# Sums of squares of two batches moved from ScalarE to TensorE, with a new order of all steps

## The chip, the cores and the metric

The kernel runs on one core of a Trainium2 chip. The metric is the time of one execution on the device in microseconds. Its engines each work through their own list of instructions in order: PE (TensorE) with its weight loads PEld, DVE (VectorE), ACT (ScalarE), POOL (GpSimd), and SP, whose queue issues all DMAs.

## The reference, cut to what matters

```python
def _attn_ref(q, k, v, n_global, n_local):        # 4 batches, 8 heads, 768 rows, 64 columns a head
    scores = (1.0 / np.sqrt(D)) * np.matmul(q, k.transpose(0, 1, 3, 2))
    keep = is_global | is_local                   # 8 first columns, and a band of 96
    scores = np.where(keep, scores + bias, -1e9)  # bias: slope of the head times the distance
    a = np.exp(scores - max)
    return np.matmul(a / (a.sum(-1, keepdims=True) + 1e-9), v)

def _moe_ref(x, w_in, w_out):                     # x: 3072 x 512, w_in: 512 x 2048, w_out: 2048 x 512
    h = x @ w_in
    g = h * erf(softplus(h))
    return g @ w_out
```

The weights come as 8-byte floats, q, k and v as 4-byte floats.

## The kernel before, in words

The rows are worked in 24 tiles of 128 (6 for each of 4 batches). Each tile goes through scores (step S), a penalty and row minimum on DVE (E), the exponential on ACT (X), a split into two 2-byte halves (eh, el), a transpose by DMA (et), the product with v (V), the division (x) and a split and transpose of the result (xh, xl, xt). Two tiles make a unit of 256 rows. A unit runs through four groups of 512 hidden columns: n = 0 to 95 counts quarters of them in the code's terms as (n, f), and the steps of group n are the up product (h, four parts), its eviction to SBUF (H), a chain of activations on ACT (t, l, i, G), products on DVE or POOL (P, Q, c, C), the split of the result (g, j) and the down product (d, eight parts), then the eviction of the output (O) and its store (o). ACT changes its function table between the steps t, G and the steps X, l, i.

All products are made of 2-byte halves, so each operand needs a scale, a power of two. For v, k and q it comes from the sum of squares of a batch: v_load brings a piece of a batch into the tile `vm` (steps vd, kd, qd), v_square squares it and adds up along the row (vq, kq, qq), v_sums adds over the partitions by a product with ones (vm), v_scale makes the scale (vp). Batch 0 has three pieces of v of 1024 columns, in tiles of tag H; each later batch has 18 pieces of 512 columns, six of v, k and q each, in one buffer of tag `vm`. For the weights w_in and w_out the same sum is bounded by a Gram product on PE and the maximum of its rows (wi_gram, gram_max; steps Wq and Wr).

The order is written out by hand as a table of steps, ORDER. Each engine executes its own instructions in the order in which the steps stand there; the table is one list for all engines, and a step is the call of one method (run_fast maps names to methods). A letter behind a step chooses the engine: a is ACT, v is DVE, p is POOL. PSUM has two buffers of tag `h`, which the up products, the transposes on PE and (later batches) v_sums share, and two of tag `o` for the down products. The profile gives nearly all instructions line 202, the line of the recording helper `Stamped`, so they are told apart by their tiles.

Of the kernel before, what the change touches and what calls it, by code (L numbers as in the profile page):

```python
# [74 lines left out]
el0,0,1 eP1,0,1 Qc2v E1,2,1 Ra7a Rc7p E1,2,0 vd0,1,3 Wq2 vd0,0,3 vq0,1,3 vq0,2,3 Wr2v Wm2 vq0,0,3 vm0 Wd4 eP1,0,0 Wh1v
ld0,2 vp0 vh0v Wl1 vl0 S2,0 Wi4a E2,0,1 Wp2 Wa4a Wc4a V0,0 V0,2 Rd12 Rd13 Ri12a Ri13p Wb4 eh1,0,1a X2,0,1 el1,0,1
eh2,0,1v el2,0,1p Wq4 Ra12a Rd2 Ri2p eh1,0,0v el1,0,0 x0 X1,2,1 eP1,2,1 Ra13a Rc13a Rd14 Ri14a E2,0,0 Ra2v Rb13 Rc2v
Ra14a Rd4 Wr4a Ri4v X2,0,0 eh2,0,0v Ra4a xP0 xh0a Rd5 va1 el2,0,0p Rc12v Wm4 eh1,2,1a S2,2 el1,2,1 E2,2,0 E2,2,1 Wh2p
xl0p ld1,2 vh1p Wd3 vl1 Wi3a Wa3a Wc3v X1,2,0 Rb12 ld3,1 TQ3 Rc14v Qc3a eP1,2,0 Wb3 Rb7 vd1,0,6 vq1,0,6 Wl2 eh1,2,0a
Rd3 ld3,0 TK3 Rc4a Rb4 Ri3a K3a V1,0 Wq3 Wr3v X2,2,0 eh2,2,0a el2,2,0v Wd5 Ra3a Rc3v Wm3 Wp3 Wh3p Wp4 ld2,2 vh2a kd1,0  # L80
Ri5a kq1,0 ld4,0 et2,0,1 S3,0 TK4 Rd15 E3,0,1 el1,2,0 qd1,0 Rb14 Wl3 Wi5a Wa5a Wc5a E3,0,0 X3,0,0 V1,2 x1 Wb5 Wq5
qq1,0 Ra5a Rc5v Rb5 Wr5v Wm5 K4a Rd0 Ri0a Ra0a Ri15p Ra15a xP1 Rb2 Wd6 Wi6a Wa6a vd1,1,6 Wh4p Rb6 Rq1 eh3,0,0a
el3,0,0p Wl4 Wd7 vq1,1,6 Rc15v ld5,0 Rb15 S3,2 Wi7p TK5 xh1v Wp5 xl1p h0,0 Rr1v Wz0 Wc6a Wb6 et2,2,0 Wh5v Wl5 X3,0,1
kd1,1 et2,0,0 X2,2,1 kq1,1 K5a Wa7a Wc7v Wq6 Wr6a eh3,0,1a Rm1 Rd1 Ra1v Ri1p qd1,1 Wm6 h0,2 Rc0a Rd8 el3,0,1v Wp6
H0,0a Rd9 Wb7 vl2 qq1,1 Rc1a eh2,2,1v el2,2,1p Ri8a Ra8a E3,2,0 X3,2,0 Rd10 Wq7 Ri10a vd1,2,6 vq1,2,6 Rp1 Ra10a ld4,1
Wr7v E3,2,1 Wm7 Wp7 Rb1 H0,2a Wh6p va2 Wl6 Ri9a Rc10v Ra9a TQ4 Rb10 Qc4a Rd11 V2,0 S4,0 Ri11v Ra11v Wz1 Rc11v Rb11
X3,2,1 kd1,2 kq1,2 et2,2,1 Rc8a Rb8 eh3,2,0a el3,2,0v Rc9a et3,0,0 qd1,2 Rb9 qq1,2 V2,2 eh3,2,1a el3,2,1p ld3,2 vh3a
et3,0,1 Rb3 Rb0 Rq3 Rr3a x2 xh2v xl2p vl3 Rq2 Rr2a Rm2 Rp2 Rh11p Rh9p vd1,3,6 E4,0,1 vq1,3,6 E4,0,0 va3 Wh7a Rq0 Rr0v
Rh8a X4,0,0 ld5,1 Rh10v Rl11 X4,0,1 kd1,3 kq1,3 et3,2,0 Rl10 Rh4a eh4,0,0a el4,0,0p ld4,2 Rl8 Rh6a Wl7 TQ5 Rm0 Rp0
vh4p Rh0p Rh7a S4,2 Qc5v E4,2,1 Rm3 Rp3 Rh5a qd1,3 qq1,3 et3,2,1 Rl9 h0,1 va4 H0,1a t0,0 Rl6 V3,0 V3,2 x3 Rh1a E4,2,0  # L90
Rl4 Rh15p vd1,4,6 vq1,4,6 vl4 Rl15 xt2 eh4,0,1a X4,2,1 el4,0,1v Rh3p et4,0,0 eh4,2,1a el4,2,1p kd1,4 kq1,4 Rh2v Rl5
ld5,2 h1,1 Rl0 et4,0,1 S5,0 E5,0,1 Rh12a h1,0 H1,0v E5,0,0 xh3v Rl1 X4,2,0 eh4,2,0v qd1,4 X5,0,0 Rl12 el4,2,0v et4,2,1
Rh13v X5,0,1 eh5,0,1v qq1,4 S5,2 va5 Rh14p Rl14 h0,3 l0,0 i0,0 E5,2,1 vd1,5,6 vq1,5,6 xl3v vh5v V4,0 H1,1a Rl7 G0,0
h1,2 et4,2,0 H0,3a kd1,5 kq1,5 Rl2 eh5,0,0v ld6,1 vl5 Rl3 t1,0 P0,0v Q0,0v el5,0,1p et5,0,1 H1,2a t0,1 h1,3 V4,2
# [5 lines left out]
H2,2v H2,3v X6,2,1 S7,0 j0,1 vq2,1,6 X6,2,0 eh6,2,0v h3,3 kd2,1 el6,2,0p et6,2,0 Kl8 d0,4 d0,5 d0,6 l2,0 Kt8 xh4a xl4p  # L100
h3,0 xt4 i1,1 E7,0,1 X7,0,1 C1,0 E7,0,0 x5 xh5v xl5v xt5 V6,0 kq2,1 g1,0a j1,0 t2,1 S7,2 vh7p vl7 d0,7 d1,0 d1,1 d1,2
eh7,0,1v ld9,0 eh6,2,1v el6,2,1p KF9v qd2,1 G1,1 G2,0 d1,3 H3,0v et6,2,1 V6,2 P1,1v el7,0,1v et7,0,1 Q1,1v Qh8a Ql8
c1,1 X7,0,0 eh7,0,0v el7,0,0p Qt8 qq2,1 ld9,1 l2,1 E7,2,0 X7,2,0 eh7,2,0a KC1,1p E7,2,1 X7,2,1 eh7,2,1a et7,0,0
el7,2,0p C1,1 g1,1a vd2,2,6 ld8,2 el7,2,1p et7,2,1 S8,0 E8,0,0 x6 E8,0,1 i2,0 X8,0,1 vq2,2,6 i2,1 et7,2,0 h3,1 j1,1
H3,1a V7,0 S8,2 kd2,2 Kh9p va8 Rl13 eh8,0,1a G2,1 P2,1p d1,4 Kl9 Kt9 d1,5 d1,6 P2,0v el8,0,1v Qh9v et8,0,1 Q2,0v kq2,2
qd2,2 vh8a Ql9 E8,2,0 H3,3v h4,0 E8,2,1 t3,0 t3,1 ld10,0 H4,0a X8,0,0 xh6v c2,0 xl6v Qt9 xt6 vl8 ld10,1 d1,7 O0,0a
V7,2 X8,2,0 Q2,1v eh8,0,0v h4,1 H4,1a o0,0 c2,1 X8,2,1 h4,2 eh8,2,1a el8,0,0v C2,1 et8,0,0 eh8,2,0a l3,1 el8,2,0v
et8,2,0 O0,1a ld9,2 S9,0 g2,1p E9,0,1 qq2,2 el8,2,1p et8,2,1 Qh10p E9,0,0 H4,2v h4,3 H4,3v C2,0 X9,0,0 va9 Kh10a g2,0p
Kl10 i3,1 l3,0 S9,2 E9,2,0 Kt10 x7 xh7a h5,1 Ql10 vd2,3,6 h5,0 Qt10 j2,0 i3,0 V8,0 V8,2 j2,1 ld11,1 X9,2,0 G3,0
# [1169 lines left out]
```

## Time and profile before

| | us |
|---|---|
| median of 3 runs | 679.18 (677.45 to 679.87) |
| profiled execution | 679.95 |
| its span, first to last instruction | 678.2 |
| PE, DVE, ACT, POOL busy | 628.6, 603.9, 618.8, 184.4 |
| mean granted clock of PE | 0.961 of full |

The busy time of an engine counts its instructions, with overlaps counted once. A matmul row's mean duration includes its passage through the array, so consecutive matmuls overlap: the time from one start to the next is what a matmul costs in a stream. Weight loads (PEld) run beside matmuls.

### The profile page before, as it was taken

How to read it: one execution, taken by the hardware profiler on the slowest of the kernel's cores; microseconds unless marked ns; L12 is line 12 of the kernel's file. 1: busy time of each engine (PE TensorE's matmuls, PEld its weight loads, DVE VectorE, ACT ScalarE, POOL GpSimd, SP SyncE). 2: the span in 40 equal slices, each digit the busy share in tenths (PEclk: the TensorE clock that was granted, in tenths of full speed). 3: DMA queues.
4: the chain of work that ended last, by engine and by line, in shares of the span. 5: the costliest groups of instructions: out<-in, count | busy, mean ns of one | idle time of the engine just before them, and what ended most of it. 6: DMA issues, size and time to landing. Idle time of an engine off the chain costs nothing.

```text
span 678.2 us, 13956 instructions
## 1 busy us (share of the span) xinstructions
PE 628.6 (93%) x5280; PEld 433.0 (64%) x5280; DVE 603.9 (89%) x1139; ACT 618.8 (91%) x875; POOL 184.4 (27%) x153
## 2 busy tenths in 40 slices
PE   4775789789999999999999999999999999999996
...
DVE  6999999999999999999999999889997989774863
ACT  5899998999999999999999999898998999999970
...
PEclk9856979999999999999999999999999999999999
...
GB/s 264 345 345 254 282 199 185 177 204 157 207 190 182 174 139 172 176 175 163 158 143 176 163 134 112 118 148 80 129 66 110 124 65 47 42 38 32 1 33 36
DMA packets 244668, 100.79 MB, mean 149 GB/s; under 512 B 225520, under 2 KB 225520, under 8 KB 244592
## 3 DMA queue, kind: packets, MB, share of 16 engines
...
## 4 chain that ended last, share of the span: by engine, by line
PE 60%; DVE 18%; ACT 8%; DMA 8%; issue 3%; POOL 1%; SPq 0%; DVEq 0%; ACTq 0%
PE h L202 27%; PE o L202 26%; DMA eT<-w 4%; PE po L202 3%; PE s L202 3%; DVE C L202 2%; DVE wo L202 2%; DVE e L202 2%; DVE raw_wo L202 2%; ACT B L202 2%; DVE w L202 1%; ACT A L202 1%; DVE A L202 1%; DVE B L202 1%; DMA vm<-in_q 1%
## 5 line engine op out<-in xcount | busy, mean ns | idle before, releaser
L202 PE MATMUL h<-xT,wi_hi 128*128 128x256 f16 x1536 | 257.0, 274 | 4.9 <-ACT H L202 2.5
L202 PE MATMUL o<-wo,g 128*128 128x512 f16 x1152 | 258.4, 379 | 1.8 <-ACT osb L202 1.3
L202 PE MATMUL h<-xT,wi_lo 128*128 128x256 f16 x768 | 210.1, 274 | 0.0
L202 PEld LDWEIGHTS <-g 128*128 128x128 f16 x1152 | 110.8, 98 | 128.3 <-issue 3.7
L202 PEld LDWEIGHTS <-wi_hi 128*128 128x128 f16 x1536 | 148.3, 98 | 33.7 <-issue 8.6
L202 POOL TENSOR_TENSOR w<-e,w 128x512 f16<-128x512 f32 (+1 forms) x43 | 56.9, 1326 | 177.9 <-DVE w L202 83.4
L202 ACT ACT_TABLE_LOAD x73 | 93.7, 1283 | 8.8 <-DVE wi_lo L686 7.5
L202 ACT ACTIVATE e<-e,mn 128x256 f32<-128x256 f32 (+1 forms) x192 | 81.9, 480 | 6.4 <-DVE mn L202 6.1
L202 PEld LDWEIGHTS <-wi_lo 128*128 128x128 f16 x768 | 75.4, 98 | 9.0
L202 DVE SCALAR_TENSOR_TENSOR g<-C,gs,g 128x1024 f16<-128x1024 f32 x48 | 67.0, 1399 | 6.5 <-POOL g L202 5.9
L202 DVE SCALAR_TENSOR_TENSOR C<-A,B 128x1024 f32<-128x1024 f32 x48 | 58.9, 1227 | 11.2 <-POOL B L202 10.4
L202 DVE CUSTOM_DVE_ANT_0 e<-s,pen,kqs 128x256 f32<-128x256 f32 (+1 forms) x144 | 59.3, 456 | 2.6 <-POOL w L202 2.2
L202 DVE TENSOR_TENSOR B<-C,B 128x1024 f32<-128x1024 f32 x43 | 54.7, 1272 | 7.1 <-POOL A L202 6.4
L202 DVE SCALAR_TENSOR_TENSOR C<-C,H 128x1024 f32<-128x1024 f32 x48 | 59.1, 1231 | 0.9
L202 ACT ACTIVATE A<-A,halves 128x1024 f32<-128x1024 f32 x48 | 54.7, 1141 | 0.2
L202 POOL TENSOR_SCALAR g<-C,gs 128x1024 f16<-128x1024 f32 x20 | 26.9, 1344 | 100.2 <-DVE C L202 84.2
L202 ACT ACTIVATE B<-A 128x1024 f32<-128x1024 f32 x48 | 50.8, 1057 | 2.9 <-DVE C L202 1.2
L202 ACT ACTIVATE B<-B 128x1024 f32<-128x1024 f32 x48 | 50.4, 1052 | 0.8
L202 PE MATMUL s<-kT,qT 64*128 64x256 f16 (+3 forms) x528 | 47.5, 311 | 3.7 <-ACT kT L202 1.4
L202 ACT ACTIVATE C<-A 128x1024 f32<-128x1024 f32 x48 | 49.9, 1051 | 0.3
L202 DVE TENSOR_TENSOR A<-A,B 128x1024 f32<-128x1024 f32 x38 | 46.3, 1220 | 4.1 <-ACT C L202 4.1
L202 ACT ACTIVATE A<-H 128x1024 f32<-128x1024 f32 x48 | 49.4, 1050 | 0.4
...
## 6 DMA issues: line engine op xcount, KB each, us to landing
...
```

The costliest lines, as they stand in the source:

```text
L202: i = getattr(self.engine, name)(*a, **k)
```

## The change

v_square has a second form, used for batches 0 and 1 (`SQ_ACT = 2`). It does not square on ACT; it reads the upper 2 bytes of each 4-byte float as a number of the 2-byte type bf16 (every second 2-byte word of the tile), cuts the tile into chunks of 64 columns (16 in a tile of 1024, 8 in one of 512) and multiplies each chunk by itself on PE, all into one 64 x 64 tile `gv` in a PSUM buffer of tag `h`. A new step (vr, kr, qr) takes the maximum of each of its rows on DVE. The sum over partitions then runs over 64 in place of 128. Batches 2 and 3 stay as they were. The table ORDER is written anew throughout: it has the same steps, with 21 new maxima, in other places, and many steps have another engine behind them (for example P: 38 on DVE and 10 on POOL before, 42 and 6 now; el: 45 on DVE and 43 on POOL before, 36 and 52 now; the output evictions O: 18 on ACT and 6 on DVE before, 14 and 10 now).

```diff
+SQ_ACT = 2
...
-el5,0,0v H1,3a qd1,5 qq1,5 xt3 X5,2,1 ld6,0 vm1 et5,0,0 c0,0 C0,0 g0,0a h3,2 vp1 Qh6a vd2,0,6 Kh6v Kl6 Ql6 eh5,2,1v
...
+vr0,0 ld2,0 TK2 K2v X0,2,1 vq0,2,3 Rd14 Ri14p Ra14a Wd2 Wc1p Wi2v Wa2a Wc2p eP1,0,1 eh1,0,1a Wb1 vr0,2 S1,2 E1,2,1
...
-        k = part.shape[1]
-        self.nc.tensor.matmul(ps[:, 0:k], self.ones, part, start=True, stop=True)
+        n, k = part.shape
+        self.nc.tensor.matmul(ps[:, 0:k], self.ones[0:n, :], part, start=True, stop=True)
...
     def v_square(self, b, i, k, z="v"):
+        t = self.vm.pop((b, i, z))
+        pe = self.fast and b < SQ_ACT
         if b not in self.a_v:
-            self.a_v[b] = self.small.tile([P, k if k == 3 else 3 * k], F32, tag=f"a_v{k}", bufs=3, name=f"a_v{b}")
-        t = self.vm.pop((b, i, z))
-        i += "vkq".index(z) * k
-        self.nc.scalar.activation(t, t, AF.Square, accum_out=self.a_v[b][:, i : i + 1])
+            self.a_v[b] = self.small.tile([D if pe else P, k if k == 3 else 3 * k], F32, tag=f"a_{'g' if pe else 'v'}{k}", bufs=1 if pe else 3, name=f"a_v{b}")
+        j = i + "vkq".index(z) * k
+        a = self.a_v[b][:, j : j + 1]
+        if not pe:
+            self.nc.scalar.activation(t, t, AF.Square, accum_out=a)
+            return
+        c = t.bitcast(BF16).rearrange("p (a b w) -> p a b w", b=D, w=2)[:, :, :, 1]
+        n = c.shape[1]
+        g = self.ps_h.tile([D, D], F32, tag="h", name=f"gv_{b}_{i}_{z}")
+        for m in range(n):
+            self.nc.tensor.matmul(g, c[:, m], c[:, m], start=(m == 0), stop=(m == n - 1))
+        self.gv[b, i, z] = (g, a)
+
+    def v_gram_max(self, b, i, z="v"):
+        g, a = self.gv.pop((b, i, z))
+        self.nc.vector.tensor_reduce(a, g, axis=AX.X, op=ALU.max)
```

Place 1 is PE in group 1 of the first unit, where its third up part (h_2) ends and its fourth (h_3) begins. `vm_4` is a piece of q of batch 1, `gv_4_q` its Gram tile, `xT` the input of the up product. Before:

```order
L202 LDWEIGHTS wi_lo
L202 MATMUL h_2_1519<-xT_525,wi_lo 128x256
L202 LDWEIGHTS wi_hi
L202 MATMUL h_3_1567<-xT_525,wi_hi 128x256
L202 LDWEIGHTS wi_hi
```

Now, with seven more pairs like the one shown at the dots:

```order
L204 LDWEIGHTS wi_lo
L204 MATMUL h_2_1603<-xT_596,wi_lo 128x256
L204 LDWEIGHTS vm_4_1633
L204 MATMUL gv_4_q<-vm_4_1633 64x64
...
L204 LDWEIGHTS wi_hi
L204 MATMUL h_3_1652<-xT_596,wi_hi 128x256
```

A Gram of eight pairs stands between two up parts that followed each other.

Place 2 is ACT while the last pieces of batch 1 are worked. `vm_4` and `vm_5` are pieces of batch 1, `a_v` takes their sums, A, B, C and H are tiles of the activation chain, `e` and `w` belong to the attention tile. Before:

```order
L202 ACTIVATE vm_4_1427,a_v_584<-vm_4_1427 128x512
L202 ACTIVATE A_1262<-A_1262,halves 128x1024
L202 ACTIVATE B_0_1478<-A_1262 128x1024
L202 ACTIVATE B_0_1478<-B_0_1478 128x1024
L202 ACTIVATE vm_5_1484,a_v_584<-vm_5_1484 128x512
L202 ACTIVATE H_0_1415<-h_1_1352,hs_836 128x512
L202 ACT_TABLE_LOAD
```

Now, at the same activations of the first group:

```order
L204 ACTIVATE A_1066<-A_1066,halves 128x1024
L204 ACTIVATE B_0_1587<-A_1066 128x1024
L204 ACTIVATE e_0_1_1590<-e_0_1_1590,mn_1492 128x256 x2
L204 ACTIVATE B_0_1587<-B_0_1587 128x1024
L204 ACTIVATE wo<-wo,swo 128x512
L204 ACTIVATE H_1_1628<-h_3_1652,hs_962 128x512
L204 ACT_TABLE_LOAD
```

The squares are gone from ACT's row there, and an exponential and a split of w_out stand between the same activations.

Place 3 is DVE at the same time, after the change only, where it takes the maxima of `gv_4_q` and `gv_5_v` into `a_v`. `vb`, `xw`, `w` and `wo` are splits into halves.

```order
L204 TENSOR_REDUCE a_v_576<-gv_4_q 64x1
L204 SCALAR_TENSOR_TENSOR wo<-raw_wo_738,swo,wo 128x512
L204 CAST xw_1649<-x_1567 128x512
L204 SCALAR_TENSOR_TENSOR vb_150<-vraw_5_1506,s_v_405,vb_150 128x8x64
L204 CAST w_0_1_1683<-e_0_1_1590 128x512
L204 TENSOR_TENSOR xw_1649<-x_1567,xw_1649 128x512
L204 TENSOR_TENSOR w_0_1_1683<-e_0_1_1590,w_0_1_1683 128x512
L204 SCALAR_TENSOR_TENSOR wo<-raw_wo_616,swo,wo 128x512
L204 SCALAR_TENSOR_TENSOR wo<-raw_wo_680,swo,wo 128x512
L204 TENSOR_SCALAR wo<-raw_wo_549,swo 128x512
L204 TENSOR_REDUCE a_v_576<-gv_5_v 64x1
```

The two maxima have nine other instructions between them. At the end of the program the last two output evictions, both on ACT before, stand one on ACT (o_1) and one on DVE (o_0).

## Rows read from the trace of the kernel before

**Rows 1.** Page, parts 1 and 2: busy shares, then the span in 40 slices.

```profile
PE 628.6 (93%) x5280; PEld 433.0 (64%) x5280; DVE 603.9 (89%) x1139; ACT 618.8 (91%) x875; POOL 184.4 (27%) x153
PE   4775789789999999999999999999999999999996
DVE  6999999999999999999999999889997989774863
ACT  5899998999999999999999999898998999999970
PEclk9856979999999999999999999999999999999999
```

**Rows 2.** Busy us by stretch: PE, PEld, DVE, ACT, POOL, PE clock, DMA share.

```profile
0.00:60.00 60.00, 37.87 (x244) 28.58 (x244) 51.41 (x152) 49.00 (x81) 16.76 (x25) 0.74 0.97 310
60.00:120.00 60.00, 47.97 (x422) 38.65 (x423) 57.13 (x147) 54.99 (x100) 19.09 (x17) 0.83 0.88 225
0.00:180.00 180.00, 139.71 (x1185) 105.59 (x1186) 166.90 (x427) 162.72 (x272) 52.72 (x58) 0.86 0.89 238
180.00:640.00 460.00, 458.31 (x3934) 311.61 (x3932) 416.69 (x696) 437.19 (x586) 127.18 (x93) 1.00 0.58 124
```

**Rows 3.** Chain that ended last: page part 4, then pieces (start, us, what).

```profile
PE 60%; DVE 18%; ACT 8%; DMA 8%; issue 3%; POOL 1%; SPq 0%; DVEq 0%; ACTq 0%
100.47 4.24 PE h L202 x24
104.71 1.46 PE po L202 x48
106.17 2.62 PE h L202 x24
```

**Rows 4.** Instruction groups by shape on ACT and DVE: busy us, mean ns, idle before.

```profile
L202 ACT ACTIVATE vm<-vm 128x1024 f32<-128x1024 f32 x3 | 3.1, 1065 | 0.0
L202 ACT ACTIVATE vm<-vm 128x512 f32<-128x512 f32 x54 | 33.6, 622 | 3.0 <-DMA vm<-in_q 2.1 <-DMA vm<-in_k 0.5 <-DMA vm<-in_v 0.2
L202 ACT ACTIVATION_READ_ACCUMULATOR vm<-vm 128x1 f32 x57 | 10.8, 190 | 0.0
L202 DVE TENSOR_REDUCE as_v<-pt_v 128x3 f32<-128x18 f32 x3 | 0.5, 169 | 0.0
L202 DVE TENSOR_REDUCE a_wi<-gr_wi 128x1 f32<-128x256 f32 x6 | 2.5, 417 | 0.0
L202 ACT ACT_TABLE_LOAD x73 | 93.7, 1283 | 8.8 <-DVE wi_lo L686 7.5
L202 ACT ACTIVATE H<-h,hs 128x512 f32<-128x512 f32 x62 | 41.0, 675 | 6.2 <-PE h L202 6.2
L202 DVE TENSOR_SCALAR H<-h,hs 128x512 f32<-128x512 f32 x34 | 25.0, 746 | 5.7 <-PE h L202 5.4
```

**Rows 5.** Timeline of PE at 74 us: start, us, instructions.

```profile
74.11 1.11 PE L202 MATMUL gr_wi<-wo 128*128 128x128 bf16 x8
76.03 0.38 PE L202 MATMUL h<-xT,wi_hi 128*128 128x256 f16 x2
```

**Rows 6.** Weight loads by shape: busy us, mean ns, idle before.

```profile
L202 PEld LDWEIGHTS <-wi_hi 128*128 128x128 f16 x1536 | 148.3, 98 | 33.7 <-issue 8.6 <-DMA xT<-xw 1.1 <-DVE xT L202 1.0
L202 PEld LDWEIGHTS <-wo 128*128 128x128 bf16 x80 | 8.6, 122 | 8.5 <-DVE wo L202 8.4
```

**Rows 7.** Waits (total us, times, longest), and tile vm up to 180 us.

```profile
PE h L202 <- ACT H L202: 2.5, 2, 2.3
  ACT vm L202: 2.0, 4
DMA to landing us min/median/max: 2.7/3.2/7.8
```

**Rows 8.** Timeline at the end: start, us, instructions, idle before.

```profile
667.29 4.92 PE L202 MATMUL o<-wo,g 128*128 128x512 f16 x22 [0.34 <-DVE g L202]
672.25 1.26 ACT L202 ACTIVATE osb<-o,gs 128x512 f32<-128x512 f32 x2 [12.16 <-PE o L202]
```

More of the change, by code (lines that the diff above doesn't have):

```diff
@@ L75 @@
[L75 to L94, printed above, removed]
@@ L100 @@
[L100 to L109, printed above, removed]
@@ new lines @@
+Rd15 Ri15a vd0,1,3 vq0,1,3 ld2,1 Ra15a Rc15a vr0,1 el1,0,1 ld0,2 vm0 vp0 TQ2 eP0,2,1 Qc2a E1,2,0 ld1,2 vh1v Wq1 Wr1a
+Wm1 S2,0 X1,2,0 vh0p vl0 Wb2 Wp1 Wh1p V0,0 Wq2 X1,2,1 eP1,2,1 eh1,2,1a eh0,2,1v el0,2,1 V0,2 eP1,0,0 eh1,0,0a Rd12
+Wr2v Wm2 E2,0,0 X2,0,0 E2,0,1 X2,0,1 el1,2,1 Rd4 x0 Wp2 vd1,0,6 Ri4p el1,0,0 eh2,0,1a eP1,2,0 eh1,2,0a el1,2,0 Rd0
+Ri0p Ra0a Rc0v Wl1 KF3p Ri12p Ra12a Rd6 Ri6a S2,2 Ra6v Wd3 Wi3a Wa3a Rd1 Wc3a va1 vq1,0,6 vl1 xP0 vr1,0 Rc14p Ra4a
+el2,0,1v xh0v kd1,0 Ra1a Rb14 Wd4 kq1,0 kr1,0 E2,2,1 Rd7 X2,2,1 V1,0 Wb3 E2,2,0 Rc4a X2,2,0 Rc12v Rb12 Rb0 Ri1p Rc1v
@@ new lines @@
+ld3,1 TQ3 ld2,2 Ri7a Ra7a Wq3 Wi4v Wr3a Rd5 eh2,0,0v el2,0,0p xl0v Ri5a Wm3 Wp3 Wh3v eh2,2,1a el2,2,1v Wh2v qd1,0
+qq1,0 qr1,0 Wl2 Rc7v Rb7 vh2a vl2 Wa4a Wc4a Wb4 ld3,0 Ra5a TK3 K3a Rb4 Wl3 Qc3a S3,0 Rd13 E3,0,1 Ri13a Ra13v Wd5 Wi5a
+Wa5a Wc5a vd1,1,6 vq1,1,6 vr1,1 E3,0,0 V1,2 et2,2,1 x1 Wb5 eh2,2,0a el2,2,0v S3,2 Rc13p Wd6 Rb13 Wi6a Rc5a Wa6a ld4,0
+TK4 Rc6v et2,0,0 Rb6 xP1 E3,2,0 Wq5 K4v Wq4 Wr5a Wr4a xh1a xl1p X3,2,0 Wm4 Wp4 Wm5 et2,0,1 Wp5 va2 V2,0 ld4,1 TQ4 Qc4a
+Wc6p Wb6 kd1,1 Rb15 X3,0,0 eh3,0,0a Rb1 kq1,1 kr1,1 Wh5a Wh4a h0,0 el3,0,0p eh3,2,0a el3,2,0p Wd7 Wz0 Wl5 E3,2,1 h0,2
@@ new lines @@
+H0,0a qd1,1 qq1,1 Wi7a Wa7v X3,2,1 qr1,1 Wc7v Rd2 et2,2,0 Wq6 Rd10 X3,0,1 Wr6a eh3,0,1a Ri2v vd1,2,6 Wb7 h0,1 Ri10a
+Ra10v Rb5 Wl4 H0,1a t0,0 Wm6 Rd11 Ra2a V2,2 ld3,2 vh3p Rd3 vq1,2,6 H0,2v kd1,2 S4,0 x2 E4,0,1 Wq7 Wr7a Wp6 Wm7 Wp7
+vr1,2 Rd8 Rd9 el3,0,1p Rc2a E4,0,0 X4,0,0 kq1,2 kr1,2 Ri3p Ra3a Ri8a Rc10a Rb2 Ri11a vl3 Ri9a Ra9a h1,0 Wz1 Rc3v Rb3
+qd1,2 qq1,2 qr1,2 H1,0a et3,0,0 Ra8v Rc8v Rb8 Rq3 Rr3a ld5,0 xh2a Rq1 Rr1a vd1,3,6 vq1,3,6 Wh6p TK5 et3,2,0 S4,2 Wl6
+Ra11a Wh7a vr1,3 Rb10 Rc9v Rb9 Rc11v xl2v Rb11 Wl7 eh3,2,1a el3,2,1v K5a et3,0,1 h0,3 H0,3a kd1,3 kq1,3 kr1,3 Rm1
```

199 lines of the change are left out of this document (108 added, 91 removed).

## The prediction

> **What bounds the kernel now.** I read the views from coarse to fine. The page's header and slices first [rows 1]: three engines carry almost the same load, PE 93%, ACT 91% and DVE 89% of the span, so nothing stands out by its share. The sums by stretch second [rows 2]: from 180 to 640 us PE is busy 458.3 of 460 us, at full clock. In the first 180 us it is busy 139.7, so 40.3 us of its idle time lie there, while DVE works 166.9 and ACT 162.7 of 180. So the front is bound by ACT and DVE, the middle by PE (which needs ACT and DVE close behind it, at 95% and 91%), and the end is short. The chain that ended last, third [rows 3]: 60% PE, 18% DVE, 8% ACT, 8% DMA. A microsecond taken from ACT in the front is worth something only if DVE, just as full there, gets shorter too; this is why the new layout of all parts counts as much as the new operation.
>
> **Removed.** 21 squares on ACT: 3 tiles of 1024 columns at 1.065 + 0.190 us and 18 of 512 columns at 0.622 + 0.190 us [rows 4], 3.8 + 14.6 = 18.4 us. All of them stood before 180 us (batch 2 squares stay on ACT).
>
> **Added.** PE: 3 x 16 + 18 x 8 = 192 pairs of weight load and matmul with 64 columns each. The trace has no such pair, so two bounds. The po matmuls are pairs with 65 moving columns and a contiguous weight tile: 48 in 1.46 us [rows 3], 30 ns a pair, 5.8 us for 192. The Gram matmuls of w_in read every fourth 2-byte word, as the new ones read every second: 8 pairs of 128 columns in 1.11 us, 139 ns a pair, and this in a place where the h matmuls beside them run at 0.38 us for two, which is the full clock [rows 5]; 192 of them are 26.7 us. The new pair has the stepped reading of the second and half its columns; I take half, 69 ns, 13.3 us, or 0.55 us for a tile of 512. All 21 tiles stand ahead of the first down product (d0,0), in the stretch with 40.3 us of PE idle time, so this hides, if PE is idle where it is put.
>
> The stepped weight loads of the Gram rows last 122 ns each against 98 ns for those of the h matmuls [rows 5, 6]. The Trainium skill (TensorE: Matmul & The Clock Gate, Weight-path perf modes — Fast Weight Load (FWL) and DoubleRow) says that the fast weight load is on only with 128 weights of a type other than FP32, so never for the new tiles of 64, and its section LDWEIGHTS (loading the stationary operand) gives columns / 1.2 ns, 53 ns for 64. That speaks against the po price of 30 ns. With 27 ns of moving columns, an estimate from that page, 192 pairs would be 15.4 us in place of 13.3 us. The trace agrees only in part: the Gram rows of w_in have 128 weights of a 2-byte type and still pay about 139 ns a pair.
>
> DVE: 21 maxima of 64 x 64 out of PSUM. Rows on either side: 169 ns for 18 columns, 417 ns for 256 [rows 4]; on the line between them 64 columns cost 0.22 us, 4.6 us in all (3.5 to 8.8). They come to the fuller engine of the front.
>
> ACT table loads: the order of ACT has 79 in place of 73, six at 1.28 us, 7.7 us [rows 4]. Up to the first product of the ninth group (d8,0) there are two more, at d16,0 eleven more: they come mostly in the middle. They are part of ACT's sums in the next part, as the squares and the maxima are.
>
> **What the new layout does to the work.** I went through both orders, gave each instruction the mean duration of its row, and summed by engine. Since rows overlap, the sums of ACT are scaled by 618.8/666.7 and those of DVE by 603.9/642.7, so that before comes to its busy time. At each place in the order, the work that ACT (or DVE) must have done, plus the PE work still to come, cannot be undercut by the end. The Gram pairs stand ahead of the places where this is largest, so their price does not enter. The largest such sum for ACT is 682.0 us before and 678.1 after, for DVE 683.9 and 680.8 (levels above the span of 678.2, since PE's rows of the front carry its low clock; only the differences are used). Four places show the spread, the sums of ACT and of DVE unscaled, then PE's work left (637.0 us in all before, 642.8 after, with pairs at 30 ns): d4,0 253.3, 254.3, 437.8 before and 245.9, 248.4, 437.8 after (about -6 us); d8,0 361.1, 358.7, 333.8 and 353.3, 358.7, 331.1 (-6, all of it ACT); d12,0 455.2, 452.9, 237.9 and 450.9, 457.1, 235.3 (-3); d16,0 536.0, 534.5, 148.0 and 529.9, 524.3, 152.8 (-3). At d3,0 and d6,0 it is +2 and +4, since the steps are ordered differently there. I take the mean of the two largest sums, **-3.5 us**; the ends are +2 and -7.
>
> **What the new waits cost.** Three kinds. (1) The tile vm has one buffer: the load of the next tile starts when the present one has been read, and lands 3.2 us later in the median, 7.8 at most [rows 7]. Before, ACT waited for it 2.0 us in all up to 180 us; now PE does, and behind a Gram on PE's queue stand scores, ups and products, and behind the waiting load on SP's queue the transposes. (2) A Gram takes one of the two PSUM buffers of tag h. Where ups and Grams alternate, the next up needs the buffer of the up before it, with only 0.55 us of Gram between, against an eviction of 0.67 to 0.75 us [rows 4]: at h1,3 and h1,1 of group 1, twice 0.2 us at least and 2.3 us at most (the longest wait of PE for H [rows 7]). (3) The buffer of a Gram comes free when DVE reaches its maximum: that of v tile 5 of batch 1 stands behind nine other DVE instructions. (1) to (3) lie between 0.4 and about 8 us; as PE has idle time there, I take **+1.0 us**, near the 2.0 that ACT paid, halved since the front's end is set by ACT and DVE.
>
> **The end.** Before, ACT evicts the last two output tiles one after the other, 1.26 us [rows 8]; now DVE takes one of them at the same time, **-0.6 us**. The chain of the last half group ends 0.34 us after PE is free, so nothing else moves there.
>
> **Sum.** The profiled execution took 679.95 us (span 678.2): 679.95 - 3.5 + 1.0 - 0.6 = 676.85. It lies 0.77 us above the median of the three runs, 679.18, so the forecast on that scale is **676.1 us**.
>
> **Rivals.** A, no change: the layout's gain is smaller than its sum says. For it: at d12,0 DVE is 4.2 us longer than before, and PE's middle is full either way, so one place with no gain is enough to set the end. Then 0 to -1 us remains: 679.0. B, slower: PE becomes the bound of the stretch in which the Grams of batch 1 stand close together. From vq1,2,6 to qq1,5, which is twelve tiles, the order gives PE 37.3 us with pairs at 30 ns, 40.7 at 69 and 46.9 at 139, against 39 us for ACT and 44 for DVE. The waits (1) to (3), 0.4 to 8 us, come on top: 41 to 55 us. From 44 us on PE decides; at 52, near the upper end, the front ends 8 us later: 679.2 - 4.1 + 8 = 683. Against it: PE stood idle 12.0 of the 60 us from 60 to 120 [rows 2], and most of the stretch lies there. C, a larger gain: granted clock in the first 120 us is 0.74 and 0.83 [rows 2], and 24 h matmuls took 4.24 us there at one place against 2.62 at the next [rows 3]. If the Grams fill PE's gaps so that this is not paid, some 4 us more come back: 672. D, that the change does not do what it says: the order has all 192 pairs and none of the 21 squares, so only the precision of the sums could differ, which costs no time.
>
> **How the numbers follow.** A measurement of this kernel can tell about 0.3%, 2.0 us, from no change, so faster means below 677.1 us and slower above 681.2. Forecast case 0.42, A 0.24, B 0.22, C 0.12. The forecast's own range is 673 to 679, by the ends of its layout term. Faster: 0.75 of the forecast case, all of C and a tenth of A, 0.46; slower: B and a little of A, 0.24; the rest, 0.30, within. The range reaches to C and B: 668 to 684.
>
> **What would show it.** Right: ACT's sum over the first 180 us falls or its work for the first groups ends some 3 to 4 us earlier; PE's stretch of full slices begins about 3 us earlier; a row of 192 gv matmuls whose stretches of 8 last about 0.55 us; PE waits for vm loads of a few us in all; ACT and DVE each evict one of the last two tiles. Wrong: PE waiting for H or for gv maxima by more than 5 us; stretches of 8 Grams over 1 us; a gap in PE in the middle, where the eleven table loads stand.

## The result, and the profile after

| | before | after |
|---|---|---|
| median, us (range; runs) | 679.82 (677.45 to 682.66; 12) | 683.56 (681.61 to 687.51; 12) |
| ratio, 95% interval | 1 | 1.0067 [1.0047, 1.0087] |
| profiled execution, its span, us | 679.95, 678.2 | 683.1, 681.3 |

The change costs 0.67%, 4.6 us; the forecast was a gain of 3.1 us. (The ratio is the one on record; the quotient of the two medians is 1.0055, 3.7 us. What follows goes by the ratios.) The page of after, parts 1 and 2 [rows 1]:

```profile
PE 628.9 (92%) x5472; PEld 435.0 (64%) x5472; DVE 610.2 (90%) x1152; ACT 615.6 (90%) x853; POOL 179.1 (26%) x153
PE   4746988789999999999999999999999999999996
DVE  5899998999999999999999999999999899779873
ACT  4789988899999999999999999999998998989980
PEclk9876998999999999999999999999999999999999
```

PE's busy time is the same as before although it has 192 pairs more: of the first eight slices of its clock two are higher (5 to 7, 7 to 9) and one is lower (9 to 8), and the mean granted clock is 0.978 in place of 0.961. The third slice of PE has fallen from 7 to 4, and in the first eight DVE and ACT show 8 at several places where they showed 9. The same by stretch, in the columns of [rows 2]:

```profile
0.00:60.00 60.00, 32.51 (x278) 25.02 (x278) 47.33 (x145) 44.81 (x76) 18.85 (x27) 0.84 0.98 296
60.00:120.00 60.00, 53.08 (x552) 44.31 (x551) 54.43 (x151) 52.93 (x88) 17.96 (x16) 0.93 0.99 240
0.00:180.00 180.00, 137.80 (x1346) 106.67 (x1347) 157.81 (x420) 154.53 (x250) 51.96 (x57) 0.92 0.94 235
180.00:640.00 460.00, 456.42 (x3946) 310.64 (x3945) 426.21 (x711) 438.78 (x583) 123.63 (x95) 1.00 0.62 125
```

Up to 180 us ACT worked 8.2 us less and DVE 9.1 us less than before, and this is no gain: both stood idle so much longer (25.5 and 22.2 us). From 60 to 120 us PE rose from 48.0 to 53.1 us. What PE waited for up to 180 us, the rows on the pieces, on H and on the rows of q (total, times, longest), of after, beside [rows 7]:

```profile
PE gv_k L204 <- DMA vm<-in_k: 8.5, 4, 3.6
PE qTp L204 <- DMA qraw<-in_q: 4.6, 2, 4.3
PE h L204 <- ACT H L204: 2.7, 2, 2.3
PE gv_v L204 <- DMA vm<-in_v: 2.3, 3, 1.4
PE gv_q L204 <- DMA vm<-in_q: 1.0, 2, 0.8
```

PE waits 11.8 us for pieces of v, k and q, where ACT waited 2.0 us before; the wait for H is nearly what it was (2.7 us, 2.5 before). The timeline of PE in after (start, us, instructions, idle before and its cause) shows where, and what a Gram costs:

```profile
58.20 2.08 PE L204 MATMUL s<-kT,qT 64*128 64x256 f32 x8 [2.25 <-ACT qT L204]
60.20 0.63 PE L204 MATMUL gv_v<-vm 128*64 128x64 bf16 x8
60.77 0.35 PE L204 MATMUL po<-va,eT 128*128 128x65 f16 x3
...
76.18 0.44 PE L204 MATMUL gv_q<-vm 128*64 128x64 bf16 x8
76.56 1.11 PE L204 MATMUL gr_wi<-wo 128*128 128x128 bf16 x8
77.49 0.40 PE L204 MATMUL h<-xT,wi_hi 128*128 128x256 f16 x2
```

From its start to the start of what follows, a Gram of eight pairs takes 0.38 us at the upper clock level, 47 ns a pair, and 0.57 us at the lower (at 60.2 us); the forecast had 69 ns. The rule of the Trainium skill that was weighed there (TensorE: Matmul & The Clock Gate, LDWEIGHTS (loading the stationary operand)), by which an estimate came to 80 ns a pair, is not borne out: 192 pairs are 9.1 us and not 15.4. A further pair costs less still: 192 more on the same tiles add 6.4 us of work (double_pairs, in the table below), 33 ns each, so part of the 47 ns is paid once for each Gram.

### The profile page after: what moved, and what is told of

Same layout as the page of the kernel before. It is cut to its first block, busy times and chain, and to the rows that moved or that the text cites. A ratio compares the mean times of both kernels' runs of the same rounds, so it can differ in the third digit from the quotient of the medians.

```text
span 681.3 us, 14307 instructions
## 1 busy us (share of the span) xinstructions
PE 628.9 (92%) x5472; PEld 435.0 (64%) x5472; DVE 610.2 (90%) x1152; ACT 615.6 (90%) x853; POOL 179.1 (26%) x153
## 5 line engine op out<-in xcount | busy, mean ns | idle before, releaser
L204 PE MATMUL h<-xT,wi_hi 128*128 128x256 f16 x1536 | 256.9, 274 | 4.2 <-ACT H L204 3.1
L204 PE MATMUL o<-wo,g 128*128 128x512 f16 x1152 | 257.4, 379 | 1.5 <-DVE g L204 1.4
L204 PE MATMUL h<-xT,wi_lo 128*128 128x256 f16 x768 | 210.1, 274 | 0.0
L204 PEld LDWEIGHTS <-g 128*128 128x128 f16 x1152 | 110.5, 98 | 129.4 <-DVE g L204 3.3
L204 PEld LDWEIGHTS <-wi_hi 128*128 128x128 f16 x1536 | 148.3, 98 | 30.5 <-issue 7.5
L204 POOL TENSOR_TENSOR w<-e,w 128x512 f16<-128x512 f32 (+1 forms) x52 | 65.0, 1254 | 167.0 <-ACT w L204 115.3
L204 ACT ACTIVATE e<-e,mn 128x256 f32<-128x256 f32 (+1 forms) x192 | 81.4, 479 | 2.6 <-DVE mn L204 2.4
L204 PEld LDWEIGHTS <-wi_lo 128*128 128x128 f16 x768 | 75.4, 98 | 9.1
L204 DVE SCALAR_TENSOR_TENSOR g<-C,gs,g 128x1024 f16<-128x1024 f32 x48 | 64.9, 1355 | 5.4 <-POOL g L204 4.9
L204 DVE SCALAR_TENSOR_TENSOR C<-C,H 128x1024 f32<-128x1024 f32 x48 | 62.2, 1298 | 1.0
L204 DVE TENSOR_TENSOR B<-C,B 128x1024 f32<-128x1024 f32 x44 | 55.9, 1276 | 7.9 <-POOL A L204 7.2
L204 DVE CUSTOM_DVE_ANT_0 e<-s,pen,kqs 128x256 f32<-128x256 f32 (+1 forms) x144 | 59.3, 455 | 3.5 <-PE s L204 1.2
L204 DVE SCALAR_TENSOR_TENSOR C<-A,B 128x1024 f32<-128x1024 f32 x48 | 61.3, 1282 | 1.3 <-POOL B L204 0.6
L204 DVE TENSOR_TENSOR A<-A,B 128x1024 f32<-128x1024 f32 x42 | 52.3, 1253 | 4.0 <-ACT B L204 2.8
L204 ACT ACTIVATE A<-A,halves 128x1024 f32<-128x1024 f32 x48 | 54.9, 1143 | 0.2
L204 ACT ACTIVATE B<-A 128x1024 f32<-128x1024 f32 x48 | 50.8, 1057 | 1.9 <-DVE C L204 0.2
L204 ACT ACTIVATE H<-h,hs 128x512 f32<-128x512 f32 x61 | 40.7, 675 | 12.3 <-PE h L204 12.3
L204 ACT ACTIVATE B<-B 128x1024 f32<-128x1024 f32 x48 | 50.5, 1052 | 0.7
L204 ACT ACTIVATE A<-H 128x1024 f32<-128x1024 f32 x48 | 49.6, 1049 | 1.3 <-DVE H L204 1.0
L204 PE MATMUL s<-kT,qT 64*128 64x256 f16 (+3 forms) x528 | 44.6, 298 | 6.5 <-DMA qT<-qw 2.5
L204 ACT ACTIVATE C<-A 128x1024 f32<-128x1024 f32 x48 | 50.0, 1052 | 0.3
```

The lines of the kernel that those rows point to most:

```text
L204: i = getattr(self.engine, name)(*a, **k)
```

## The experiments

Six theories were put to the test. W: PE's waits for the pieces cost the time. G: the PSUM buffer that a Gram holds until DVE has taken its maximum delays what follows. P: PE is the bound and each pair pushes the end. C: the pairs cost nothing, since they keep PE's clock at the upper level. L: the new layout is not worth what was forecast. E: the end has become longer. Ratios are to runs of the kernel before that were taken at the same time as the kernel's own; the row of before is of those beside two_one. Where a kernel has another table of the order its lines have other numbers (L185 for L204).

| kernel | median us | ratio, interval | mean clock, all runs | span | work | lost | idle |
|---|---|---|---|---|---|---|---|
| before | 678.8 | 1 | 0.960 | 678.2 | 608.0 | 20.6 | 49.6 |
| after | 683.56 | 1.0067 [1.0047, 1.0087] | 0.974 | 681.3 | 619.9 | 9.0 | 52.5 |
| other_data | 679.51 | 1.0015 [0.9996, 1.0034] | 0.972 | 677.1 | 617.8 | 13.7 | 45.5 |
| one_pair | 683.67 | 1.0070 [1.0046, 1.0094] | 0.962 | 680.6 | 613.1 | 20.5 | 47.0 |
| double_pairs | 685.61 | 1.0103 [1.0067, 1.0140] | 0.974 | 681.2 | 626.3 | 9.5 | 45.5 |
| floor | 683.04 | 1.0054 [1.0032, 1.0076] | 0.965 | 683.8 | 611.9 | 23.9 | 48.0 |
| other_double | 680.38 | 1.0020 [1.0002, 1.0037] | 0.980 | 677.9 | 629.7 | 4.4 | 43.7 |
| two_buffers | 678.66 | 0.9985 [0.9964, 1.0007] | 0.975 | 674.9 | 619.9 | 9.4 | 45.7 |
| two_one | 683.04 | 1.0054 [1.0029, 1.0079] | 0.966 | 679.1 | 613.0 | 17.1 | 48.9 |
| before_two | 677.10 | 0.9970 [0.9949, 0.9990] | 0.959 | 678.2 | 608.6 | 18.6 | 50.9 |
| before_warm | 686.68 | 1.0089 [1.0060, 1.0117] | 0.964 | 686.6 | 617.2 | 18.6 | 50.7 |

The last four columns are worked out from the profiled execution: span = PE's work at the upper clock level + what it lost at the lower + its idle time. Half of PE's busy time at the lower level counts as lost, since a group of three h matmuls starts every 0.64 us there and every 0.33 us at the upper level, as the timeline of floor shows across the rise:

```profile
74.71 0.64 PE L204 MATMUL h<-xT,wi_hi 128*128 128x256 f16 x2
75.14 0.42 PE L204 MATMUL h<-xT,wi_lo 128*128 128x256 f16 x1
75.35 0.64 PE L204 MATMUL h<-xT,wi_hi 128*128 128x256 f16 x2
...
77.67 0.38 PE L204 MATMUL h<-xT,wi_hi 128*128 128x256 f16 x2
77.89 0.27 PE L204 MATMUL h<-xT,wi_lo 128*128 128x256 f16 x1
78.00 0.38 PE L204 MATMUL h<-xT,wi_hi 128*128 128x256 f16 x2
```

A profiled execution may lie 2 or 3 us off its kernel's median, so the spans are not compared with each other to the last microsecond; the ratios are.

**other_data**: the Grams read a constant tile, so no Gram waits for the load of a piece.

```diff
-        c = t.bitcast(BF16).rearrange("p (a b w) -> p a b w", b=D, w=2)[:, :, :, 1]
-        n = c.shape[1]
+        n = t.shape[1] // D
+        c = self.ident.bitcast(BF16).rearrange("p (a b w) -> p a b w", b=D, w=2)[:, :, :, 1]
...
-            self.nc.tensor.matmul(g, c[:, m], c[:, m], start=(m == 0), stop=(m == n - 1))
+            self.nc.tensor.matmul(g, c[:, m % 2], c[:, m % 2], start=(m == 0), stop=(m == n - 1))
```

> The changed kernel, but its 192 Gram pairs read a constant tile in SBUF in place of the piece that was loaded (so the sums are those of the constant); loads, order and maxima stay. Theory W (PE waits in order for loads into the one vm buffer, 11.8 us in its profile, and scores, transposes and ups stand behind it): without the wait the time falls by 4 to 7 us, to 677 to 680. Theory L (the new layout is itself slower on the chip, by where it puts weight loads and table loads): no change, 682 to 685. Theory G (the PSUM buffer that a Gram holds until DVE's maximum delays the ups): no change either, since Gram and maximum stay.

Measured 0.52% below after, 3.5 us. W holds: the waits are worth several us. G by itself would have left the time as it was, since Grams and maxima stay. The gain of 4.1 us that the forecast had without the waits is not there.

**new_order_act** and **old_order_gram**: one half of the change each. The first has the new order and squares on ACT, without Grams and maxima; the second the old order with Grams in place of the squares and each maximum right behind its Gram.

```diff
-SQ_ACT = 2
+SQ_ACT = 0
```

> The new order with all squares on ACT as before, and no Grams and maxima: the layout by itself. ACT gets 18.4 us of squares back at places of the order where the layout left no room for them. Theory W: the layout by itself, given that room, would be worth -3.5; with the squares put back ACT's front is 18 us longer, shared with what ACT now idles for (25 us in the first 180), so 684 to 692. Theory L: the layout is bad with or without Grams, 688 to 696.

> The old order with the Grams on PE where the squares stood on ACT, each maximum right behind its Gram: the operation by itself. Theory W: PE waits for its loads at places that were chosen for ACT, over 10 us in all, and the 18.4 us that ACT is rid of come to little: 679 to 684. Theory L: the operation is good by itself and the layout spoils it: 674 to 678. Theory G: PE waits for PSUM buffers of tag h, by over 3 us, seen in the waits of PE h and gv for DVE.

Measured 702.4 (ratio 1.0345 [1.0314, 1.0376]) and 709.92 (1.0472 [1.0434, 1.0511]). Both lie above all that was expected (684 to 696, and 674 to 684). Neither half stands alone: an order is written for its operations, and with others the queues block. In the new order with squares PE waited 12.3 us for sums of ACT, and the DMA queue 53.8 us for squares (25.7 before). In the old order with Grams PE waited 10.4 us for pieces, as W had it, and 6.7 us for maxima that held the buffer of a transpose or an up product (4.1 and 2.6), over the 3 us that G had named. The halves say little of the parts of the change, and this way of splitting it failed.

**early_loads**: two buffers for the pieces of batch 1 (the tile of tag osb, free until the first output, by turns with vm), and each load moved in the order to stand right behind the Gram two before it, which frees its buffer. The moves are left out here:

```diff
-            t = self.xp.tile([P, n], F32, tag="vm", name=f"vm_{b}_{i}")
+            j = 3 * i + "vkq".index(z)
+            t = self.xp.tile([P, n], F32, tag="osb" if b == 1 and j % 2 else "vm", name=f"vm_{b}_{i}")
```

> The changed kernel with two buffers in turn for the pieces of batch 1 (the second is that of the output tile, not in use until the first output), and each load put in the order right behind the Gram two before it. Theory W: the waits of PE for vm go from 11.8 to under 3 us, and the time falls by 3 to 6 us, to 678 to 681. Theory L: the waits go and the time stays within 1.5 us of 683.6. A third way: the earlier loads push the weights' loads back in a DMA queue that is full (share 0.90 to 1.03 from 20 to 140 us), and the waits only change their name.

Measured 709.18, ratio 1.0445 [1.0418, 1.0472], far above all that was expected. The DMA queue and PE, some rows up to 180 us:

```profile
SPq L185 <- PE gv_v L185: 22.1, 5, 7.0
SPq L185 <- PE gv_q L185: 14.7, 4, 5.1
SPq L185 <- PE gv_k L185: 10.5, 4, 5.0
```

```profile
PE qTp L185 <- DMA qraw<-in_q: 8.6, 2, 5.2
PE kTp L185 <- DMA kraw<-in_k: 7.1, 2, 6.6
PE gv_k L185 <- DMA vm<-in_k: 4.6, 1, 4.6
```

PE waited 4.6 us for pieces in place of 11.8, but the queue, which goes in order, now stood 47 us at loads whose buffer was not free yet, and the rows of q and k behind them came late. So a load issued early into a buffer that was still in use held up all that followed it.

**two_buffers**: the same second buffer, with the order of after left as it is.

> The kernel after, the pieces of batch 1 by turns in the buffer of tag vm and in that of the output evictions (unused until 198 us); the order is the same, loads too, but a load need not wait for the Gram ahead of it. If the single buffer is what makes the loads late: most of the 11.8 us that TensorE waited for them goes, 680 to 681.5, ratio 1.002 to 1.005. If the loads are late because the DMA queue as a whole is (busy share 0.94 to 1.03 from 20 to 120 us): 683 to 684.5, ratio 1.005 to 1.008.

Measured 0.82% below after, 5.6 us: the gain of the first theory, and more than it said. What PE waited for, some rows:

```profile
PE qTp L204 <- DMA qraw<-in_q: 3.6, 2, 3.4
PE gv_k L204 <- DMA vm<-in_k: 3.0, 3, 1.4
PE gv_k L204 <- DVE a_v L204: 2.7, 1, 2.7
PE kTp L204 <- DVE a_v L204: 2.0, 1, 2.0
```

11.8 us of waiting for pieces have become 3.0, and of the sum in the table the idle time alone has changed, by 6.8 us; work is the same and the loss by the clock nearly so. So with all 192 pairs the single buffer makes the difference between a slower kernel and one like before. (other_data, in which no Gram waits for a piece, lies 0.30% above two_buffers; it lost 13.7 us at the lower level against 9.4.)

**before_two**: the kernel before with that second buffer.

> The kernel before with the second buffer of the run two_buffers: the pieces of batch 1 by turns in the buffer of tag vm and in that of the output evictions. If the wait for the single buffer came with the change: no difference, 678.5 to 680.5, ratio 0.998 to 1.002. If it stood in the kernel before as well (its DMA queue waited 25.7 us for squares of ACT up to 180 us): 673 to 676, ratio 0.990 to 0.995, and two_buffers would not be a remedy for what the change brought.

Measured 0.3% below before, 2.0 us, between the two. The wait stood in the kernel before as well, at a third of its later price; some 3.6 of the 5.6 us came with the change. This is also the fastest kernel of the case, the only one whose interval lies below 1; with equal buffers the change costs 0.15%, which is no difference that these runs can tell.

**q_first, two_q and two_q_max**: the load of the q rows of tile 3 is moved ahead of a load of 1 MB and one of 512 KB, in after and in two_buffers; in the third one maximum stands right behind its Gram as well. Shown are stretches of the table, not whole lines of it.

```diff
-Ra1a Rb14 Wd4 kq1,0 kr1,0 E2,2,1 Rd7 X2,2,1 V1,0 Wb3 E2,2,0 Rc4a X2,2,0 Rc12v Rb12 Rb0 Ri1p Rc1v ld3,1
+Ra1a Rb14 ld3,1 Wd4 kq1,0 kr1,0 E2,2,1 Rd7 X2,2,1 V1,0 Wb3 E2,2,0 Rc4a X2,2,0 Rc12v Rb12 Rb0 Ri1p Rc1v
...
-vq1,0,6 vl1 xP0 vr1,0
+vq1,0,6 vr1,0 vl1 xP0
```

> The kernel after with one step moved: the load of the q rows of tile 3 stands ahead of the 1 MB load of w_in (part 4) and the 512 KB load of w_out on the DMA queue, not behind them. Its transpose on TensorE waited 4.30 us for it at 48.9 us. If a wait of TensorE in the front reaches the end: 679.5 to 681.5, ratio 1.000 to 1.003. If the queue only passes the lateness to the next load (that w_in part comes about 1 us later for its Gram): 683 to 684.5, ratio 1.005 to 1.008.

> The run two_buffers with the load of the q rows of tile 3 ahead of the 1 MB load of w_in and the 512 KB load of w_out, as in q_first. TensorE waited 3.44 us for these rows at 47.6 us. If that wait reaches the end now that the loads of the pieces don't stand in the way: 675 to 677.5, ratio 0.993 to 0.997. If it is passed on to the next load, as in q_first: 678 to 680, ratio 0.998 to 1.001.

> The run two_q with one maximum moved: that of the first piece of v of batch 1 stands right behind its Gram in the order, ahead of two steps of DVE. Its Gram ended at 39.4 us in two_buffers and its maximum began at 42.63, and the next Gram but one step waited 2.74 us for the PSUM buffer until then. If a PSUM buffer kept by a late maximum reaches the end: 0.5 to 2 us below two_q. If DVE sets that stretch: within 0.5 us of two_q.

Measured 683.61 (1.0068 [1.0041, 1.0094]), 678.36 (0.9993 [0.9971, 1.0014]) and 677.97 (0.9984 [0.9963, 1.0006]): nothing that the runs can tell each time. The wait for the q rows went, and others took its place; of q_first, some rows of PE up to 180 us:

```profile
PE pt_wi L185 <- ACT gr_wi L185: 7.5, 4, 5.0
PE gv_k L185 <- DMA vm<-in_k: 7.3, 3, 3.4
PE s L185 <- ACT qT L185: 3.1, 1, 3.1
```

The weights passed over come later, and one of their sums (pt_wi) 5.0 us later than wanted (2.5 us in four waits in after). Not every wait of PE in the front reaches the end. What a late maximum costs was not tested by two_q_max: the wait of 2.7 us for it in two_buffers had already become one of 3.1 us for the piece of k in two_q, and with the maximum moved it was 3.6 us for that piece.

**one_pair and double_pairs**: only the first pair of each Gram (21 in all), or all of them twice (384).

```diff
-        for m in range(n):
-            self.nc.tensor.matmul(g, c[:, m], c[:, m], start=(m == 0), stop=(m == n - 1))
+        for m in range(1):
+            self.nc.tensor.matmul(g, c[:, m], c[:, m], start=(m == 0), stop=(m == 0))
```

> The kernel after, but each Gram multiplies only the first of its 8 (16) chunks of 64 columns: 21 pairs in place of 192; loads, waits for loads, order, buffers and maxima stay. It leaves out most of the sums of squares of batches 0 and 1. Theory P (TensorE is the bound once the queue of work has begun, 456.4 of 460 us busy from 180 to 640, so that each Gram pair put in front pushes the end): 171 pairs go at 31 to 47 ns each, 5 to 8 us, so 676 to 678.5, the ratio to the kernel before 0.995 to 1.000. Theory W (only the waits of TensorE for the loads cost, and the pairs fill time in which it is idle anyway): 682.5 to 684, ratio 1.005 to 1.008.

> The kernel after, but each Gram goes over its chunks twice, 384 pairs in place of 192 (the sums are doubled, so scales are at most one power of two smaller); all else stays. Theory P: 192 more pairs at 31 to 47 ns, 6 to 9 us, so 689 to 692, ratio 1.014 to 1.019. Theory W: most of the pairs run where TensorE is idle anyway, 683.5 to 685, ratio 1.006 to 1.009.

Without 171 pairs the time is the same within 0.2 us (1.0070 against 1.0067); 192 more cost 0.36%, which the runs can hardly tell from nothing, by 6.4 us of work, between the two expectations. P falls. W's numbers are met, but not for its reason (that the pairs fill idle time): PE's work is 6.8 us less and its idle time 5.5 us less, and what is saved goes into the clock, 11.5 us more lost at the lower level. PE also waited only 3.5 us for pieces here, and nothing was gained by it: the 11.8 us of after belong to a PE that comes to the pieces early.

**floor, other_double and two_one**: one pair, or 384, on the constant tile; and two_buffers with one pair a Gram.

> The kernel after, each Gram cut to one pair on a constant tile: neither a wait of TensorE for a load nor work of its own but 21 pairs; loads, order and maxima stay, the sums of squares of batches 0 and 1 are left out. This is the new layout alone, without squares on any engine. If the layout is worth what was forecast for it (3.5 to 4 us) and the squares are gone from ACT for nothing: 673 to 675, ratio 0.992 to 0.995. Theory L (the layout is worth nothing, since the front is set by the DMA queue, 0.9 to 1.03 busy up to 120 us): 678 to 680, ratio 0.999 to 1.002.

> The run other_data with 384 pairs on the constant tile in place of 192. Theory C (the pairs cost 31 ns each on TensorE, but keep its granted clock at the upper level for longer: 65.7 us at the lower level with 21 pairs, 42.0 with 192): low-level time falls to 30 to 36 us and the time stays within 1.5 us of other_data, 678.5 to 681, ratio 1.000 to 1.004. Theory P (each pair pushes the end): plus 6 us, 685 to 686, ratio 1.009 to 1.011.

> The run two_buffers with each Gram cut to its first pair (21 pairs in place of 192); most of the sums of squares of batches 0 and 1 are left out. Theory C (pairs cost 31 to 33 ns each on TensorE, but without them it runs longer at its lower clock level): low-level time rises from 31.5 us to 45 or more, and the time stays at 677 to 680, ratio 0.998 to 1.002. Theory P (with the waits for loads gone TensorE is the bound and each pair pushes the end): 5.5 us less, 672 to 674, ratio 0.990 to 0.993.

Taking pairs away makes the kernel slower where the Grams wait little or not at all for loads: floor lies 0.39% above other_data and two_one 0.69% above two_buffers, 4.7 us, with 6.9 us less work on PE. That is the direction of C, and more than C said, which had the time unchanged. Both by stretch of 20 us, two_one first, then two_buffers:

```profile
20.00:40.00 20.00, 15.76 (x107) 11.77 (x105) 16.14 (x56) 14.00 (x31) 11.05 (x10) 0.75 1.03 344
40.00:60.00 20.00, 7.96 (x57) 6.28 (x57) 19.82 (x40) 19.94 (x29) 2.63 (x2) 0.59 0.99 296
60.00:80.00 20.00, 18.75 (x163) 15.19 (x160) 18.82 (x48) 17.71 (x29) 6.90 (x4) 0.81 1.04 244
```

```profile
20.00:40.00 20.00, 16.74 (x164) 13.12 (x162) 17.49 (x59) 15.77 (x33) 11.40 (x10) 0.83 1.04 344
40.00:60.00 20.00, 8.52 (x81) 6.59 (x80) 19.83 (x39) 19.85 (x27) 2.44 (x2) 0.62 1.07 322
60.00:80.00 20.00, 18.35 (x195) 15.54 (x193) 19.59 (x50) 17.93 (x30) 7.41 (x4) 0.96 1.06 256
```

From 60 to 80 us PE is nearly full in both, so there its clock counts: 0.81 against 0.96. Before, PE was busy 13.85 us in that stretch. The mean clock over all runs, 0.975 against 0.966, goes the same way as the two profiles. But by the table the clock is not the whole of it: without the pairs PE has 6.9 us less work, loses 7.7 us more at the lower level and stands idle 3.3 us more. The clock alone gives back little more than the pairs cost; the rest is that about half of their time would have been idle time. No run holds the clock fixed, so the split is read from the profiles and not measured by itself. (The 384 pairs of other_double bring the clock to 0.980 and leave the time, 0.05% above other_data: the gain is used up.)

**before_warm**: the old order with 16 constant pairs ahead of each of the twelve transposes of q and k of tiles 0 to 5, squares on ACT.

```diff
...
+            for m in range(16):
+                self.nc.tensor.matmul(ps[0:D, 0, 0:D], c[:, m % 2], c[:, m % 2], start=(m == 0), stop=(m == 15))
```

> The kernel before with 16 Gram pairs on a constant tile ahead of each of the twelve transposes of k and q rows of tiles 0 to 5 (192 pairs, into the PSUM tile that the transposes then overwrite); squares stay on ACT. TensorE of the kernel before ran 54.3 us at its lower clock level, 30.7 of them from 28.5 to 59.3. If the lower level there reaches the end of the old order as it does in the new: less than 40 us at the lower level and 673 to 676, ratio 0.993 to 0.997. If DVE and ACT set that stretch (28.2 and 28.7 of 30 us busy) and the clock of TensorE doesn't: 677.5 to 680, ratio 0.999 to 1.003.

Measured slower by 0.89%, which neither side expected: PE got 9.2 us more work and only 2.0 us back from the clock. The likely reason is that these pairs stand right ahead of transposes that others wait for; pairs are not free wherever they are put.

**old_const**: the contents of other_data in the old order, to get the layout's worth by the difference.

> The order of the kernel before with the contents of the run other_data: no squares on ACT for batches 0 and 1, in their place 192 Gram pairs on a constant tile (no wait for loads), each with its DVE maximum right behind it; the loads stay. It leaves out the sums of squares of these two batches. Beside other_data (679.5) it tells what the new layout is worth with the same work in both. Layout worth what was forecast (3.5 us): 682.5 to 684, ratio 1.006 to 1.009. Layout worth nothing: 679 to 680, ratio 1.001 to 1.003. Layout a loss: below 678, ratio under 1.000, since ACT has lost some 15 us of work here against the kernel before.

Measured 699.74 (1.0291 [1.0263, 1.0318]), outside all that was expected. DVE waits 6.2 us for Grams of v, for its maxima stand right behind them; ACT waits 8.8 us for ups. What the layout is worth with equal contents stays unmeasured.

**two_tail**: two_buffers with the last two stores exchanged.

```diff
-O11,1a o11,1 O11,0v o11,0
+O11,1a O11,0v o11,0 o11,1
```

> The run two_buffers with the last two stores exchanged: the store of the tile that DVE evicts (ready 0.6 us earlier) stands first on the DMA queue. From the end of the last product to the program's end two_buffers took 6.63 us. If the wait of the first store behind the second tile is what lengthens the end: 5.7 to 6.1 us there. If not: 6.4 to 6.8. The time as a whole can't tell 0.6 us: 676 to 680, ratio 0.996 to 1.001.

The end of after:

```profile
669.77 4.92 PE L204 MATMUL o<-wo,g 128*128 128x512 f16 x22
674.08 0.75 DVE L204 TENSOR_SCALAR osb<-o,gs 128x512 f32<-128x512 f32 x1 [4.37 <-PE o L204]
674.73 0.69 ACT L204 ACTIVATE osb<-o,gs 128x512 f32<-128x512 f32 x1 [12.16 <-PE o L204]
675.44 1.28 SPq L204 DMA_DIRECT2D out<-osb  x2
```

The evictions end 0.73 us after the last product, 1.30 before [rows 8]. But the tile that is ready first, DVE's at 674.83, is stored second; both stores begin behind ACT's. From the end of the last product (674.69) to the program's end it takes 6.62 us, before 5.94. In two_tail the first store begins with DVE's end and this stretch is 5.97 us, against 6.63 in two_buffers:

```profile
668.55 0.75 DVE L185 TENSOR_SCALAR osb<-o,gs 128x512 f32<-128x512 f32 x1 [4.37 <-PE o L185]
669.20 0.69 ACT L185 ACTIVATE osb<-o,gs 128x512 f32<-128x512 f32 x1 [12.16 <-PE o L185]
669.33 1.42 SPq L185 DMA_DIRECT2D out<-osb  x2
```

E holds. The time as a whole (679.27, 1.0003 [0.9976, 1.0030]) can't tell 0.6 us.

## Why the prediction was wrong

Two terms of the sum failed, the new waits and the layout. With two buffers in both kernels the change costs 1.0 us (two_buffers less before_two), where the sum had -4.1 for layout and end; the single buffer brings 3.6 us more, where the sum had +1.0 for new waits. So the layout is the larger miss. Split by pairs, the 4.6 us are: the new layout with 21 pairs and two buffers 3.7 us slower (two_one), the other 171 pairs 4.7 us faster (two_buffers less two_one), the single buffer 5.6 us slower (after less two_buffers). These terms depend on each other: with 21 pairs the second buffer is worth only 1.1 us (one_pair less two_one), within the noise, and with the single buffer the pairs are worth nothing that the runs can tell.

**The new waits** failed in size. The working put kinds (1) to (3) between 0.4 and 8 us and took 1.0, "near the 2.0 that ACT paid, halved". Measured, the second buffer is worth 5.6 us, 3.6 of them new. The price of before was the wrong neighbour: ACT read the pieces where they had come anyway, PE reads them in an order in which 11.8 us are waited for. Halving it because the front is set by ACT and DVE failed too: both waited along, 8 to 9 us more idle time in the front. Of the three kinds it was (1). For (2) the wait for H went from 2.5 to 2.7 us; (3) was there, 1.4 us in after and 2.7 us at one place of two_buffers, and what it cost was not measured. The prediction's list of signs did not catch this: it took waits for vm of a few us as a sign of being right, and PE waiting for H or for maxima by more than 5 us as one of being wrong; neither that nor a gap in the middle came.

**The layout term**, -3.5 us, failed as well. It added ACT's or DVE's work done and PE's work left, in durations of the trace of before. Such a sum says what the end cannot undercut; it leaves out every wait, and the difference of two such bounds was taken for a difference of times. Of that gain nothing is seen in floor and two_one, 0.54% slower than before though ACT has shed its 18.4 us of squares there, and 0.15% are in two_buffers. What the sum could not see is that in the new order PE is nearly full from 60 to 80 us, so that its clock counts there. After in two stretches, then before in the first of them:

```profile
60.00:80.00 20.00, 19.06 (x193) 16.39 (x192) 19.43 (x48) 18.36 (x30) 6.37 (x4) 0.89 1.03 275
80.00:100.00 20.00, 17.09 (x183) 14.18 (x182) 18.23 (x45) 17.59 (x29) 3.61 (x4) 1.00 0.94 250
60.00:80.00 20.00, 13.85 (x106) 11.72 (x107) 19.65 (x36) 18.24 (x32) 4.01 (x3) 0.83 0.90 269
```

From 80 to 140 us PE is full in neither. A weak sign over many runs: among the 12 runs of two_buffers, time and mean clock have a correlation of -0.84, the strongest in the table (-0.38 in after, -0.20 in floor); among the runs of the kernel before, in five sets of 17 to 29, it lies between -0.13 and +0.24. Why the layout brought nothing stays open: that the clock is the reason is argued, not shown, as old_const gave no clean comparison.

**Rival C** had the mechanism of the clock: the clock of the first 60 us rose from 0.74 to 0.84, of the next from 0.83 to 0.93, and with the second buffer the pairs pay for themselves with 4.7 us over. It was forecast as a gain on top, and went into making up for a slower layout. **Rival B** had the time, 683, in part by luck: PE as the bound of the Gram stretch through pairs and waits. The waits were right; that pairs push the end was not (one_pair). Its stretch, from the third piece of v of batch 1 to the last of q, took 47.7 us in after (81.1 to 128.8) and 44.0 in two_buffers (80.6 to 124.6), with nearly the same busy time of PE; B had set its price at 52. The two stretches, after first:

```profile
81.00:128.50 47.50, 39.22 (x432) 32.05 (x428) 41.80 (x112) 41.95 (x68) 12.87 (x13) 0.96 0.95 205
80.50:124.40 43.90, 39.03 (x432) 32.09 (x428) 40.93 (x112) 41.02 (x66) 12.45 (x13) 0.96 0.98 217
```

So 3.7 of the 5.6 us of the single buffer lie there, and they are for the most part idle time of all three engines.

**The price of a pair**, 69 ns, was too high by a third, with no effect on the sum. Part of that is a misread row: 1.11 us for eight pairs of a Gram of w_in is the row's length, and from its start to the start of the next row (75.05 us, pt_wo) it is 0.94 us, 117 ns a pair and not 139. Two smaller slips: the three sums of B differ by the price of 88 pairs, eleven tiles and not twelve; and a layout term from -7 to +2 us gives a range of 672.6 to 681.6 us, not 673 to 679. **Maxima** (0.21 us each, forecast 0.22) and **table loads** (79) were right. **The end** was forecast 0.6 us shorter and became 0.7 us longer: the eviction gained its 0.57 us, and the order of two stores on one queue lost more.
